# First mixture of experts: experts taken in order of their token counts, four small ones packed into one place

## The chip, the core and the metric

One NeuronCore of a Trainium2 chip runs the whole program. The metric is the device time of one execution in microseconds (us); the median of three runs of the kernel before is 952.01 us (951.53 to 958.26). TensorE is PE in the profile (PEld its weight loads), VectorE is DVE, ScalarE is ACT, GpSimd is POOL, SyncE is SP. SP does no arithmetic here: it issues nearly all weight transfers, in the order of the program.

## What is computed

```python
attn_out = _attn_ref(**attn_kwargs)          # block-causal attention, 4 x 8 heads x 576 x 64
x = attn_out.transpose(0, 2, 1, 3).reshape(2304, 512)
x = _moe_ref(x=x, **moe_kwargs)              # first mixture
return _moe2_ref(x=x, **moe2_kwargs)         # second mixture

def _moe_ref(x, w_skip, w_gate, w1, w2):     # top 1 of 8 experts, some tokens skipped
    do_compute = x @ w_skip > 0
    xc = x[do_compute]
    e_idx = np.argmax(xc @ w_gate, axis=1)
    ...                                      # gate_w: softmax at e_idx
    for e in range(E):
        mask = e_idx == e
        h = np.maximum(xc[mask] @ w1[e], 0.0)          # 512 -> 1024
        y[mask] = gate_w[mask, None] * (h @ w2[e])     # 1024 -> 512
    out[do_compute] = xc + y
```

The second mixture routes every token to two of eight other experts of the same size, with noise added to its router. Everything is float32. Computed from the reference's inputs, 806 tokens enter the first mixture; the experts get 8, 10, 122, 180, 460, 16, 2 and 8 of them.

## The kernel before, in words

The work has three stages on one instruction stream per engine, in an order that the program writes out by hand (`tc.manual_schedule()`): attention; then the first mixture, one *place* of 128 tokens after another; then the second mixture with 592 places per expert. Each row that leaves the first mixture goes through the second router in the place after it.

**Between attention and the first mixture** PE works for the second mixture: `up` and two `down` calls (256 early tokens of expert 0). Woven into them through the `between` arguments are the last steps of the first router (`begin`, `go_on`, `last`), which end with GpSimd scatters of (token, gate) into the list `l1` in DRAM, and `table` and `fullest`, which read the list back, rank the experts (DVE `key`, `keyx`, `keyi`), read two expert numbers into SP registers (`values_load`) and gather more of the list (`ctm`).

**First mixture.** `places` has twelve entries of 128 tokens: one for each expert, three more for the fullest expert and one more for the second fullest (`FULL, NEXT = 3, 1`). An expert's weights are eight transfers of 512 KB: four chunks of the first matrix (to `ring`, three buffers of 2 MB, used as they are) and four of the second (to `ST[4:8]`), which ACT and DVE split into a high and a low part (`W2`, two buffers); the low part of chunk 7 is GpSimd's. Ten expert loads are made (`order`), 40 MB; the first expert's are fixed, so they are issued while attention ends.

One place (`tile1`) on PE is: `cut` (transposes the next place's gathered rows, L161 and ACT L893), `gemm1` half 0 (L1041, f32) with `turn` (L161) and `mm` (L1080) of the second router between, `gemm1` half 1, with the router's `second` steps put in front of the relu (ACT L1045, DVE L1046), and `gemm2` (L1055 to L1057, 24 fp32r products of 512 columns), with the router's `third` after its fifth group. `finish` (DVE L1095 to L1099) writes the rows. On DVE `second` has the line L290 (`atb`); on GpSimd the low part of chunk 7 is L1162; gathers and scatters are L202 and L194.

What exceeds the places is left to a loop behind the second mixture (`one_more`), under a branch that is not taken with these inputs.

Instructions of one engine run in program order, and an engine waits at the first whose operands are not ready. A tile pool opened later on the same memory (`rp`, over `ep`) waits until the old tiles are released: the ring's buffers lie over `x0`, `h0` and `y` of the `up` and `down` calls.

Of the kernel before, what the change touches and what calls it, by code (L numbers as in the profile page):

```python
# [22 lines left out]
E = 8  # L23
# [6 lines left out]
FULL, NEXT = 3, 1  # L30
# [16 lines left out]
def moe_kernel(ctx, tc, q, k, v, w_skip, w_gate, w1, w2, w_gate2, w_noise, noise, w1b, w2b, out):  # L47
# [54 lines left out]
    npad = fiota("npad", [P, 1], [[0, 1]], N, 1)  # L102

# [781 lines left out]
    with ExitStack() as bctx:  # L885
# [11 lines left out]
        with ExitStack() as ectx:  # L897
# [18 lines left out]

            def split0(c):
                raw_split(ST[c], Q0, c, nc.scalar, nc.vector)
                raw_load(ST[c], w1, w2, 1, c)

            Q0 = Obj()
            Q0.w2h, Q0.w2l = Q2
            xg_pool = []
# [9 lines left out]
            def last():  # L933
                counted.extend(counts(C1, "n1"))
                late.L = L[B - 1][:, :, 9:25]
                late.nz = cst.tile([P, 5, E], F32, name="latenz")
                nc.vector.tensor_copy(late.nz, X[B - 1][:, :, D:W])
                late.inv = skip[B - 1]
                late.tok = tok_of(B - 1)
                xctx.close()  # L940
                xg = bctx.enter_context(tc.tile_pool(name="xg", bufs=1, side="right", reuse_waits="tile"))
                x = xg.tile([P, 6, D], F32, name="xg")
                XG.extend(x[:, i, :] for i in range(6))
                x_.append(x)
                nc.gpsimd.memset(x[:, 0:3, :], 0.0)
                lists.append(list_load(l1, 1, x[0:E, 3, :]))

            late, counted, XG, lists, x_ = Obj(), [], [], [], []
            up(WA, x0, h0, ((0, H0),), {1: begin, 2: lambda: go_on(3), 3: last, 4: lambda: split0(KC),
                                        5: lambda: split0(KC + 1), 7: lambda: split0(KC + 2)})  # L950
            tables = []

            def table():
                tok1, idx1, gate1, val1 = token_table(lists[0], 1, "t1", "s")
                nc.gpsimd.memset(x_[0][:, 3:5, :], 0.0)
                for e in range(2):
                    gather(xd, idx1[:, 0, e:e + 1], XG[e], N)
                inv1 = cst.tile([P, 1, E], F32, name="inv1")
                nc.vector.tensor_scalar(inv1, val1, -BIG, BIG, op0=OP.mult, op1=OP.add)
                tables.extend(t[:, 0, :] for t in (tok1, idx1, gate1, inv1))  # L960
                fullest()

            more, fuller = [], []

            def fullest():
# [7 lines left out]
                ni = cst.tile([P, 2], I32, name="fulli")  # L973
                nc.vector.tensor_copy(ni, ki[:, 0:2])
                fuller.extend(nc.values_load(ni[0:1, i:i + 1], engines=(mybir.EngineType.SP,), min_val=0, max_val=E - 1)
                              for i in range(2))
                nf = cst.tile([P, 2], F32, name="fullf")
                nc.vector.tensor_copy(nf, ki[:, 0:2])
                begun = cst.tile([P, E], F32, name="begun")
                own = cst.tile([P, E], F32, name="own")  # L980
                nc.vector.memset(begun, float(P))
                n = FULL + NEXT
                base = cst.tile([P, 2], F32, name="seatb")
                seat = cst.tile([P, n], I32, name="seats")
                for i, tiles_ in enumerate((FULL, NEXT)):
                    nc.vector.tensor_scalar(base[:, i:i + 1], nf[:, i:i + 1], float(R), posc, op0=OP.mult, op1=OP.add)
                    for t in range(tiles_):
                        c = i * FULL + t
                        nc.vector.tensor_scalar(seat[:, c:c + 1], base[:, i:i + 1], float((t + 1) * P), None, op0=OP.add)
                ctm = cst.tile([P, n, 2], F32, name="ctm")  # L990
                for c in range(n):
                    gather(l1, seat[:, c:c + 1], ctm[:, c, :], NROW)
                for i, tiles_ in enumerate((FULL, NEXT)):
                    nc.vector.tensor_scalar(own, e8, nf[:, i:i + 1], float(tiles_ * P), op0=OP.is_equal, op1=OP.mult)
                    nc.vector.tensor_tensor(begun, begun, own, op=OP.add)
                tokm, gatem, invm = (cst.tile([P, n], F32, name=nm + "m") for nm in ("tok", "gate", "inv"))
                idxm = cst.tile([P, n], I32, name="idxm")
                more.extend((begun, ctm, tokm, idxm, gatem, invm))

            def further():  # L1000
# [8 lines left out]
            down(WA, h0, 0, P, known[1][1][:, 0, :], known[1][2][:, 0, :], ep,  # L1009
                 {1: lambda: split0(KC + 3), 3: table})  # L1010
            tok1, idx1, gate1, inv1 = tables
            n1f, n1i = counted
            down(WA, h0, P, P, known[1][1][:, 1, :], known[1][2][:, 1, :], ep, {6: lambda: cut(0, 0, 0)})
        rp = bctx.enter_context(tc.tile_pool(name="rp", bufs=1, reuse_waits="tile"))
        ring = [ST[0:KC]] + [tiles(rp, f"r{i}", KC, F32) for i in range(2)]
        order = [0, 1, 2, fuller[0], 3, 4, 5, fuller[1], 6, 7]
        V = len(order)
        W1 = [ring[i % 3] for i in range(V)]
        places = []
        for j in range(V):  # L1020
            if j in (3, 7):
                for t in range(NEXT if j > 3 else FULL):
                    T = Obj()
                    T.j, T.work = j, t == 0
                    c = t + (FULL if j > 3 else 0)
                    T.gate, T.tok, T.idx, T.inv = (more[i][:, c:c + 1] for i in (4, 2, 3, 5))
                    places.append(T)
            else:
                T = Obj()
                T.j, T.work = j, True  # L1030
                T.gate, T.tok, T.idx, T.inv = (a[:, order[j]:order[j] + 1] for a in (gate1, tok1, idx1, inv1))
                places.append(T)


        def gemm1(j, e, half, between={}):

            s = bank("s", 2 * j + half).rearrange("p (i n) -> p i n", i=4)
# [62 lines left out]

        def tile1(i):

            T = places[i]
            j, k = T.j, i % 2
            work = split_steps(j) if T.work else {}
# [6 lines left out]
            turn, mm, first, second, third = pending(row1, k > 0)  # L1112
# [22 lines left out]
            if j == V - 1:  # L1135
                for c in range(KC):
                    raw_load(ST[c], w1b, w2b, 1, c)
            finish(o, XG[i % 3], T.gate, T.tok, T.idx, T.inv)
# [13 lines left out]
        def split_steps(e):  # L1152

            def step(c):
                src = ST[c].rearrange("p (a d) -> p a d", a=2)
                h, l = (W2[e % 2][i][c - KC] for i in range(2))

                def hi():
                    nc.scalar.activation(h, src, AF.Copy)

                def lo():
                    (nc.gpsimd if c == NCH - 1 else nc.vector).tensor_sub(l, src, h.bitcast(F32))  # L1162

                def load():
                    if e + 2 < V:
                        raw_load(ST[c], w1, w2, order[e + 2], c)
                    else:
                        raw_load(ST[c], w1, w2b, e + 2 - V, c)
                    if 1 <= e < V - 2:
                        raw_load(W1[e + 2][c - KC], w1, w2, order[e + 2], c - KC)  # L1170
                return {"hi": hi, "lo": lo, "load": load}
            return {c: step(c) for c in range(KC, NCH)}

        for c in range(KC):
            raw_load(W1[1][c], w1, w2, 1, c)
        for c in range(KC):
            raw_load(W1[2][c], w1, w2, 2, c)

# [37 lines left out]
        further()  # L1216
        for i in range(len(places)):
            if i == len(places) - 2:
                settled.append(len(put_back))
            if i + 1 < len(places):  # L1220
                cut((i + 1) % 3, (i + 1) % 2, 0)
            if i + 2 < len(places):
                take(places[i + 2].idx, (i + 2) % 3)
            if i == 4:
                over = rest()
            tile1(i)
# [262 lines left out]
```

## Time and profile before

| | |
|---|---|
| median of three runs | 952.01 us |
| profiled execution | 954.42 us, span 952.6 us |
| busy share PE / DVE / ACT / POOL | 93% / 56% / 39% / 45% |
| granted TensorE clock, mean | 0.966 |
| attention and what is woven into it | 0 to 278 us |
| `up`, `down` for the early tokens | 278 to 308.5 us |
| first mixture, twelve places | 308.5 to 510.2 us |
| second mixture | 510 to 952 us |

A granted clock of 1.00 is TensorE's level of 2.4 GHz, 0.50 its level of 1.2 GHz. Times in the rows are counted from the start of the span. Matmul ends are modelled, so the distance from one start to the next tells more than a row's length.

### The profile page before, as it was taken

Reading aid. Unit: us, or ns where it says so; the run is one execution under the profiler, and the core shown is the slowest. Engines: PE = TensorE matmul, PEld = TensorE weight load, DVE = VectorE, ACT = ScalarE, POOL = GpSimd, SP = SyncE. Lnnn points to the kernel's source line nnn. Section 1 sums busy time; section 2 is a strip of 40 time slices with the busy share of each in tenths; the row PEclk is TensorE's granted clock in tenths of the full one; section 3 lists DMA queues with packets and bytes.
Section 4 is the critical chain, followed back from the end, with each engine's and each line's share of the span. In section 5 each row is a group of like instructions: output and inputs, shape, how many; then the busy total and the mean of one; then the engine's idle time right before and its main releaser. Section 6 shows DMA issues by size and latency. Waiting matters only on the chain.

```text
span 952.6 us, 16785 instructions
## 1 busy us (share of the span) xinstructions
PE 887.7 (93%) x6184; PEld 784.5 (82%) x6184; DVE 537.1 (56%) x1464; ACT 370.1 (39%) x664; POOL 433.4 (45%) x326
## 2 busy tenths in 40 slices
PE   6998998898789988899999999999999999999995
PEld 4777776676678877678788899999999999999994
DVE  4666756746355577255766464555546364555631
ACT  4565554544333433133433162242434233343400
POOL 1223254242226546535545341554828465570835
PEclk9999999988799999899997999999999999999998
DMA  6776378351154878338866272564645455560333
GB/s 99 155 148 153 82 153 137 75 119 34 45 207 141 279 277 262 49 112 265 264 199 200 46 226 67 142 123 124 143 104 123 98 141 105 135 144 1 27 34 43
DMA packets 161243, 125.77 MB, mean 132 GB/s; under 512 B 110784, under 2 KB 124864, under 8 KB 161152
## 3 DMA queue, kind: packets, MB, share of 16 engines
q1 hardware_dynamic: 136272, 100.34, 37.6%
q0 software_dynamic: 22448, 23.98, 14.8%
q8 instruction: 50, 0.82, 0.4%
q10 hardware_dynamic: 2432, 0.30, 0.2%
q14 instruction: 41, 0.34, 0.1%
HBM read 104.93 MB, written 23.51 MB: 135 GB/s over the span
## 4 chain that ended last, share of the span: by engine, by line
PE 77%; DVE 11%; issue 3%; ACT 3%; SPq 3%; DMA 2%; another core or an unknown queue 0%; POOLq 0%; DVEq 0%; POOL 0%; ACTq 0%
PE bank L403 22%; PE sums L635 6%; PE bank L1041 5%; PE bank L446 4%; PE bank L447 4%; PE bank L448 4%; PE bank L1285 4%; PE bank L1287 4%; PE bank L1286 4%; PE bank L607 3%; PE seta L556 2%; PE bank L387 2%; DVE atb L290 2%; PE bank L1057 2%; PE bank L701 2%
## 5 line engine op out<-in xcount | busy, mean ns | idle before, releaser
L1295 POOL DMA_INDIRECT out_dram<-y,toq x77 | 150.6, 1956 | 94.3 <-DVE y L1294 75.1
L403 PE MATMUL bank<-xh,w1h 128*128 128x296 f32 (+2 forms) x512 | 123.1, 301 | 0.0
L403 PE MATMUL bank<-xl,w1h 128*128 128x296 f32 (+2 forms) x512 | 122.1, 299 | 0.7 <-DVE xl L391 0.3
L403 PE MATMUL bank<-xh,w1l 128*128 128x296 f32 (+2 forms) x512 | 122.2, 300 | 0.0
L406 ACT ACTIVATE hh<-bank 128x296 fp32r<-128x296 f32 (+2 forms) x128 | 47.8, 413 | 149.2 <-PE bank L403 145.8
L635 PE MATMUL sums<-v,ptS 128*128 128x65 f32 x640 | 94.1, 283 | 9.9 <-remote 5.1
L407 DVE SCALAR_TENSOR_TENSOR hl<-bank,hh 128x296 fp32r<-128x296 f32 (+2 forms) x128 | 54.1, 459 | 77.1 <-ACT hh L406 74.0
L635 PEld LDWEIGHTS sums<-v,ptS 128*128 128x128 f32 x640 | 84.2, 199 | 12.2 <-remote 5.2
L403 PEld LDWEIGHTS bank<-xh,w1h 128*128 128x128 f32 x512 | 88.4, 191 | 0.9 <-ACT xh L390 0.2
L403 PEld LDWEIGHTS bank<-xl,w1h 128*128 128x128 f32 x512 | 87.8, 191 | 1.2 <-DVE xl L391 1.2
L497 ACT ACTIVATE ptS<-bank 128x384 f32<-128x384 f32 (+2 forms) x119 | 56.1, 511 | 82.8 <-PE bank L607 38.9
L403 PEld LDWEIGHTS bank<-xh,w1l 128*128 128x128 f32 x512 | 87.8, 191 | 0.0
L149 ACT ACTIVATE q2h<-st 128x1024 fp32r<-128x1024 f32 x32 | 62.2, 1945 | 61.6 <-PE bank L448 61.6
L202 POOL DMA_INDIRECT rows<-xd,t3x x35 | 35.6, 1018 | 86.0 <-PE bank L387 79.0
L194 POOL DMA_INDIRECT l<-ent,idxb x40 | 42.8, 1070 | 67.3 <-DVE C L185 33.3
L1285 PE MATMUL bank<-hh,q2h 128*128 128x336 f32 x224 | 72.3, 323 | 0.0
L1287 PE MATMUL bank<-hh,q2l 128*128 128x336 f32 x224 | 70.9, 317 | 0.0
L1286 PE MATMUL bank<-hl,q2h 128*128 128x336 f32 x224 | 70.8, 316 | 0.0
L152 DVE TENSOR_TENSOR q2l<-st,q2h 128x1024 fp32r<-128x1024 f32 x32 | 61.2, 1913 | 16.6 <-ACT q2h L149 16.6
L607 PEld LDWEIGHTS bank<-idf,P 128*128 128x128 f32 x320 | 36.4, 147 | 32.2 <-issue 19.1
L446 PE MATMUL bank<-q2h,hh 128*128 128x512 f32 x136 | 54.7, 402 | 0.0
L447 PE MATMUL bank<-q2l,hh 128*128 128x512 f32 x136 | 54.3, 399 | 0.0
(348 smaller groups left out, 1958.2 us busy)
## 6 DMA issues: line engine op xcount, KB each, us to landing
st<-in_moe_w_dram SPq DMA_DIRECT2D x124, 512.0 KB
r<-in_moe_w_dram SPq DMA_DIRECT2D x24, 512.0 KB
out_dram<-zero SPq DMA_DIRECT2D x19, 256.0 KB
kraw<-in_k_dram SPq DMA_DIRECT2D x60, 72.0 KB
qraw<-in_q_dram SPq DMA_DIRECT2D x60, 72.0 KB
v<-in_v_dram SPq DMA_DIRECT2D x64, 64.0 KB
xd<-Xe SPq DMA_DIRECT2D x2, 1024.0 KB
out_dram<-y,toq POOLq DMA_INDIRECT x77
```

What stands on the lines that cost most here:

```text
L149: nc.scalar.activation(h, src, AF.Copy)
L152: on_low.tensor_sub(l, src, h.bitcast(F32))
L403: nc.tensor.matmul(s[i][:, :c1 - c0], a, part[:, c, c0:c1], start=st, stop=sp)
L446: nc.tensor.matmul(o[:n], a, wh, start=f == 0, stop=False)
L447: nc.tensor.matmul(o[:n], a, wl, start=False, stop=False)
L497: nc.scalar.activation(o, i, AF.Copy)
L607: nc.tensor.transpose(pt[:, c:c + P], U.P[:, h, c:c + P], idf)
L635: nc.tensor.matmul(o[:, h, t, :], U.T[h][:, c + j * P:c + (j + 1) * P], vb[:, j, h, :], start=j == 0, stop=j == t)
L1285: nc.tensor.matmul(o[:, :n], wh, a, start=f == 0, stop=False)
L1286: nc.tensor.matmul(o[:, :n], wh, b, start=False, stop=False)
L1287: nc.tensor.matmul(o[:, :n], wl, a, start=False, stop=f == FC - 1)
L1295: st = nc.gpsimd.indirect_dma_start(out=out.rearrange("n (a d) -> (n a) d", d=P), in_=y, in_offset=None, compute_op=OP.add, out_offset=bas ...
```

## The change

The first mixture gets nine places. All eight experts are ranked by count (`ranking`, called in `last`), and the ranks are read into eight SP registers. The four fullest experts get 4, 2, 1 and 1 places (`TILES`); the other four share one place, 32 tokens each (`FEW`), whose products are f32 matmuls of 32 stationary columns, one per expert, written to PSUM partitions 0 to 31, 32 to 63, 64 to 95 and 96 to 127. The shared place's work is eight `few_step` calls, of eight matmuls of 512 columns each: steps 0 to 4 stand between `gemm1` and `gemm2` of places 1 to 4 (`middle`), steps 5 to 7 in `few_place`, which is the seventh of the nine. Their weights (16 MB) come unsplit through `fewb`, `ST[4:8]` and `W1b`. Expert 0's fixed early loads are gone; the first expert's eight loads stand behind the `values_load`s. All nine token lists come by gather (`ctm`), with the three first row gathers in `further`, now inside the first `down`. In `tile1` the relu of half 1 stands in front of `second`, `third` moves one group later, and GpSimd's low part of chunk 7 is made in four pieces.

```diff
-FULL, NEXT = 3, 1
+TILES = (4, 2, 1, 1)
+FEW = 32
...
-            for c in range(T0, NCH):
-                raw_load(ST[c], w1, w2, 0, c)
             for t in range(T0):
                 turn2(x0, ST[t], t * P, P, "s")
-            for c in range(T0):
-                raw_load(ST[c], w1, w2, 0, c)
...
-                nc.gpsimd.memset(x[:, 0:3, :], 0.0)
-                lists.append(list_load(l1, 1, x[0:E, 3, :]))
+                ranking()
+                nc.gpsimd.memset(x[:, 0:4, :], 0.0)
...
+                rank.extend(nc.values_load(ni[0:1, i:i + 1], engines=(mybir.EngineType.SP,), min_val=0, max_val=E - 1)
+                            for i in range(E))
+                for c in range(NCH):
+                    raw_load(ST[c], w1, w2, rank[0], c)
...
+                for c in [0, 1, n - 1] + list(range(2, n - 1)):
+                    gather(l1, seat[:, c:c + 1], ctm[:, c, :], NROW)
...
+                for c, g in ((0, 0), (1, 1), (sum(TILES), 3)):
+                    gather(xd, idxm[:, c:c + 1], XG[g], N)
+
+            up(WA, x0, h0, ((0, H0),), {1: begin, 2: lambda: go_on(3), 3: last})
...
+            down(WA, h0, 0, P, known[1][1][:, 0, :], known[1][2][:, 0, :], ep, {4: further})
+            down(WA, h0, P, P, known[1][1][:, 1, :], known[1][2][:, 1, :], ep, {3: reached, 7: lambda: cut(0, 0, 0)})
...
+        W1b, fewb = (tiles(rp, f"r{i}", KC, F32) for i in range(2))
+        few = rp.tile([P, FC, P], F32, name="few")
+        W1 = [ST[0:KC], W1b, ST[0:KC], W1b]
+        fewbuf = [fewb, ST[KC:], ST[KC:], fewb, ST[KC:], ST[KC:], fewb, W1b]
...
+        def few_step(i):
+            if i in (0, KC):
+                sums[:] = [bank("s", 2 + half) for half in range(2 if i == 0 else 1)]
+            for half in range(2):
+                for g in range(P // FEW):
+                    cols = slice(g * FEW, (g + 1) * FEW)
+                    f = i if i < KC else 2 * (i - KC) + half
+                    nc.tensor.matmul(sums[half if i < KC else 0][cols], few[:, f, cols],
+                                     fewbuf[i][g][:, half * 512:half * 512 + 512], start=f == 0,
+                                     stop=f == (KC if i < KC else FC) - 1, skip_group_check=True)
...
+                    for a in range(2):
+                        for d in (slice(0, D // 2), slice(D // 2, D)):
+                            nc.gpsimd.tensor_sub(l[:, a, d], src[:, a, d], h[:, a, d].bitcast(F32))
...
+        splits = {0: lambda: split_steps(ST[KC:], 1, lambda c: few_chunk(1, c)),
+                  2: lambda: split_steps(fewb, 0, lambda c: few_chunk(3, c)),
+                  4: lambda: split_steps(fewb, 1, lambda c: few_chunk(6, c)),
+                  7: lambda: split_steps(fewb, 0, lambda c: None),
+                  8: lambda: split_steps(ST[KC:], 1, lambda c: raw_load(ST[c], w1, w2b, 1, c))}
...
+        def middle(i):
+            if i == 0:
+                few_rows()
+            if i == 1:
+                few_step(0)
+                seconds(1, fewb)
+                few_step(1)
+                load_few(2)
+            if i == 2:
+                few_step(2)
+                load_few(4)
+            if i == 3:
+                few_step(3)
+                few_relu()
+                seconds(2, fewb)
+                load_first(2, ST[0:KC])
+            if i == 4:
+                few_step(4)
+                load_few(5)
+            if i == 5:
+                load_few(7)
...
-            gemm1(k, j, 1, {3: second})
+            gemm1(k, j, 1)
+            second()
             extra(i)
-            o = gemm2(j, {4: third})
-            pick("lo", 6)
+            if i == 0:
+                pick("lo", 6)
+            middle(i)
+            o = gemm2(j, {5: third})
+            if i > 0:
+                pick("lo", 6)
...
+        def few_place(i):
...
+            turn()
+            few_step(5)
+            for c in range(KC, NCH):
+                raw_load(ST[c], w1, w2b, 0, c)
+            mm()
+            first()
+            few_step(6)
+            seconds(3, fewb)
+            second()
+            few_step(7)
+            load_first(3, W1b)
...
-        for c in range(KC):
-            raw_load(W1[1][c], w1, w2, 1, c)
-        for c in range(KC):
-            raw_load(W1[2][c], w1, w2, 2, c)
+        load_few(0)
+        load_first(1, W1b)
```

`seconds(j, buf)` and `load_first(j, buf)` load the second and first matrix of the expert of rank j (four chunks each), `load_few(i)` one 512 KB chunk of each of the four small experts. `few_rows` and `few_turn` transpose the shared place's rows and its hidden layer, `few_relu` is its relu.

## Rows read from the trace of the kernel before

**Rows 1.** The page, shares of the span and the chain that ended last.
```profile
PE 887.7 (93%) x6184; PEld 784.5 (82%) x6184; DVE 537.1 (56%) x1464; ACT 370.1 (39%) x664; POOL 433.4 (45%) x326
PE 77%; DVE 11%; issue 3%; ACT 3%; SPq 3%; DMA 2%; another core or an unknown queue 0%; POOLq 0%; DVEq 0%; POOL 0%; ACTq 0%
```
**Rows 2.** Windows, one per place: stretch, length, busy per engine (instructions), clock, DMA share, GB/s.
```profile
308.51:324.88 16.37, 15.18 (x107) 13.26 (x106) 11.25 (x35) 6.62 (x11) 9.73 (x7) 1.00 0.86 267
...
357.71:376.00 18.29, 15.81 (x114) 13.61 (x113) 14.94 (x62) 6.67 (x12) 10.66 (x8) 1.00 0.80 280
376.00:398.05 22.05, 18.47 (x108) 14.61 (x107) 6.05 (x35) 3.01 (x7) 13.04 (x14) 0.85 0.35 75
398.05:412.73 14.68, 14.68 (x108) 13.35 (x106) 5.60 (x31) 2.90 (x7) 6.63 (x7) 1.00 0.25 38
412.73:431.28 18.55, 16.72 (x107) 14.37 (x106) 10.94 (x34) 6.58 (x11) 8.58 (x8) 0.91 0.56 183
...
sum 201.72, PE 186.49 PEld 161.73 DVE 123.66 ACT 71.76 POOL 107.27; mean PE 15.54 PEld 13.48 DVE 10.30 ACT 5.98 POOL 8.94
```
**Rows 3.** Timeline of the first place: start, length, engine, line, tiles, shapes, count, [idle before].
```profile
312.95 0.96 PE L1080 MATMUL bank<-wcat,xt 128*128 128x16 f32 x8
313.77 3.82 PE L1041 MATMUL bank<-xt,st 128*128 128x128 f32 x32
317.34 0.48 PE L1055 MATMUL bank<-q2h,ht 128*128 128x512 f32 x1
321.57 0.50 PE L1055 MATMUL bank<-q2h,ht 128*128 128x512 f32 x1 [1.19 <-ACT ht L1045]
318.17 2.54 POOL L1162 TENSOR_TENSOR w2l<-st,w2h 128x1024 fp32r<-128x1024 f32 x1 [2.19 <-ACT w2h L1159]
318.91 1.81 DVE L290 TENSOR_TENSOR atb<-mib,pinv 128x2 f32<-128x2 uint32 x1
320.83 0.20 ACT L295 ACTIVATE e<-d 128x1 f32<-128x1 f32 x1 [2.75 <-DVE d L291]
```
**Rows 4.** PE's waits, 295 to 520 us: who waited for whom, total, times, longest.
```profile
PE bank L1055 <- ACT ht L1045: 8.8, 8, 1.8
```
**Rows 5.** Timeline in attention: products that fill only part of TensorE's columns.
```profile
69.52 0.89 PE L652 MATMUL sums<-v,ptS 128*64 128x65 f32 x18
70.16 0.45 PE L562 MATMUL setb<-kt,qt 64*64 64x288 f32 x1
71.37 0.87 PE L607 MATMUL bank<-idf,P 128*128 128x128 f32 x6
```
**Rows 6.** Timeline ahead of the first mixture: router list, ranking, gathers.
```profile
288.34 0.17 PE L338 MATMUL bank<-C,onesb 128*128 128x8 bf16 x1
293.82 1.16 POOL L194 DMA_INDIRECT l<-ent,idxa  x1 [0.30 <-issue]
296.24 0.34 SPq L362 DMA_DIRECT2D xg<-l  x1
300.72 0.17 DVE L974 CAST fulli<-keyi 128x2 int32<-128x2 uint32 x1
302.36 0.82 SPq L131 DMA_DIRECT2D r<-in_moe_w_dram  x2
307.02 1.01 POOL L202 DMA_INDIRECT ctm<-l,seats  x1 [0.30 <-issue]
309.60 0.17 DVE L1003 COPY tokm<-ctm 128x4 f32<-128x4 f32 x1
```
**Rows 7.** POOL's waits, 295 to 520 us.
```profile
POOL l L194 <- DMA next<-l,seat: 3.8, 1, 3.8
```
**Rows 8.** Windows of 16 to 18 us and of 4 us, columns as in the second group.
```profile
310.00:328.00 18.00, 16.81 (x124) 14.89 (x123) 11.13 (x36) 6.82 (x12) 10.77 (x8) 1.00 0.93 307
497.00:514.00 17.00, 15.04 (x103) 13.16 (x101) 12.30 (x42) 7.17 (x12) 11.00 (x9) 0.96 0.53 155
392.00:396.00 4.00, 4.00 (x11) 2.14 (x10) 1.50 (x8) 0.60 (x1) 0.00 (x0) 0.50 0.00 0
```

More of the change, by code (lines that the diff above doesn't have):

```diff
@@ L944, in last, with ranking @@
                 x_.append(x)
-                nc.gpsimd.memset(x[:, 0:3, :], 0.0)
-                lists.append(list_load(l1, 1, x[0:E, 3, :]))
[L948 to L965, printed above, removed]
+                ranking()
+                nc.gpsimd.memset(x[:, 0:4, :], 0.0)
+            late, counted, XG, x_ = Obj(), [], [], []
+            more, rank = [], []
+            def ranking():
                 key = cst.tile([P, E], F32, name="key")
@@ L972, in fullest @@
                 nc.vector.max_index(ki, kx, key)
[L973 to L978, printed above, removed]
+                ni = cst.tile([P, E], I32, name="ranki")
@@ L980, in fullest @@
                 own = cst.tile([P, E], F32, name="own")
[L981 to L994, printed above, removed]
+                nc.vector.memset(begun, 0.0)
+                for i in range(E):
+                    nc.vector.tensor_scalar(own, e8, nf[:, i:i + 1], float(TILES[i] * P if i < len(TILES) else FEW),
+                                            op0=OP.is_equal, op1=OP.mult)
@@ L995, in fullest @@
                     nc.vector.tensor_tensor(begun, begun, own, op=OP.add)
[L996 to L998 removed]
+                more[0] = begun
             def further():
@@ L1029, in moe_kernel @@
+        few = rp.tile([P, FC, P], F32, name="few")
+        W1 = [ST[0:KC], W1b, ST[0:KC], W1b]
+        fewbuf = [fewb, ST[KC:], ST[KC:], fewb, ST[KC:], ST[KC:], fewb, W1b]
+        V = len(TILES)
+        places = []
+        for j, tiles_ in enumerate(TILES):
+            for t in range(tiles_):
                 T = Obj()
-                T.j, T.work = j, True
-                T.gate, T.tok, T.idx, T.inv = (a[:, order[j]:order[j] + 1] for a in (gate1, tok1, idx1, inv1))
+                T.j, T.d, c = j, len(places), len(places)
+                T.x, T.xT = XG[c % 3], c % 2
+                T.gate, T.tok, T.idx, T.inv = (more[i][:, c:c + 1] for i in (4, 2, 3, 5))
@@ L1032, in moe_kernel, with load_first, load_second, load_few @@
                 places.append(T)
+        T = Obj()
+        T.j, T.x, c = None, XG[3], len(places)
+        T.gate, T.tok, T.idx, T.inv = (more[i][:, c:c + 1] for i in (4, 2, 3, 5))
+        dense = list(places)
+        places.insert(sum(TILES[:2]), T)
+        def load_first(j, buf):
+            for c in range(KC):
+                raw_load(buf[c], w1, w2, rank[j], c)
+        def load_second(j, buf, c):
+            raw_load(buf[c - KC], w1, w2, rank[j], c)
+        def load_few(i):
+            for g in range(P // FEW):
+                raw_load(fewbuf[i][g], w1, w2, rank[V + g], i)
@@ L1101, in tile1, with after @@
+        def after(i):
+            if i == 3:
+                few_turn()
+            if i == 7:
+                for c in range(KC):
+                    raw_load(ST[c], w1b, w2b, 1, c)
         def tile1(i):
             T = places[i]
-            j, k = T.j, i % 2
-            work = split_steps(j) if T.work else {}
+            j, k = T.j, T.xT
+            work = splits[i]() if i in splits else {}
             def pick(kind, *cs):
@@ L1110, in pick @@
                         work[c][kind]()
-            turn, mm, first, second, third = pending(row1, k > 0)
+            turn, mm, first, second, third = pending(row1, i % 2 > 0)
             gather(noise, T.idx, nz, N)
@@ L1129, in tile1 @@
             pick("lo", 7)
-            gemm1(k, j, 1, {3: second})
+            gemm1(k, j, 1)
+            second()
             extra(i)
-            o = gemm2(j, {4: third})
-            pick("lo", 6)
-            pick("load", 7, 6)
-            if j == V - 1:
-                for c in range(KC):
-                    raw_load(ST[c], w1b, w2b, 1, c)
-            finish(o, XG[i % 3], T.gate, T.tok, T.idx, T.inv)
+            if i == 0:
[4 more added lines that the diff above has]
+                pick("lo", 6)
+            pick("load", 7, 6)
+            after(i)
+            finish(o, T.x, T.gate, T.tok, T.idx, T.inv)
+        def few_place(i):
+            T = places[i]
+            turn, mm, first, second, third = pending(row1, i % 2 > 0)
+            gather(noise, T.idx, nz, N)
+            turn()
+            few_step(5)
+            for c in range(KC, NCH):
+                raw_load(ST[c], w1, w2b, 0, c)
[6 more added lines that the diff above has]
+            load_first(3, W1b)
+            extra(i)
+            third()
+            finish(sums[0], T.x, T.gate, T.tok, T.idx, T.inv)
         def rest():
```

108 lines of the change are left out of this document (61 added, 47 removed).

## The prediction

> **What bounds the kernel now.** I read the page first: PE is busy 93% of the span and carries 77% of the chain that ended last [rows 1]. So time is gained where PE does less, or where it stands. Then the windows of the twelve places: they take 201.7 us, 186.5 of them busy on PE [rows 2]. A place without splitting takes 14.68 us with PE never idle; one with splitting 16.37, of which 1.19 is PE waiting in `gemm2` [rows 2, 3]. That wait occurs eight times, 8.8 us in all, always for the relu of half 1 [rows 4]. Its cause is order: ACT's little exponential of the router (L295) stands in front of the relu, waits for DVE's `atb`, and that takes 1.81 us beside GpSimd's 2.54 us subtraction [rows 3]. Three places are out of the pattern: 18.29 us where the router of the last 640 tokens burdens DVE (14.94 us busy), 22.05 and 18.55 us where PE stood or ran slowly [rows 2]. Transfers reach 307 GB/s at a 0.93 share and are asked for at 155 GB/s near the end [rows 8], so they don't bound the stage now.
>
> **Dense places.** Eight instead of twelve. Places 1, 3 and 5 split nothing: 3 x 14.7. Places 0, 2, 4, 7 and 8 split: 16.37 less the 1.19 wait, 15.2, five times. With the relu in front, ACT no longer waits for `atb`; what is late next is `ohb` for `third`, which has one more group of `gemm2` before it and, with four GpSimd pieces, a shorter block on `atb`. I take no wait. The late router stays where it was, with an excess of 18.29 - 16.4 = 1.9. Sum 44.1 + 76.0 + 1.9 = 122.0 us. The cutting in pieces adds a few starts on GpSimd, which is busy 8.9 of 16.8 us per place [rows 2]; they lie beside PE's work.
>
> **The shared place.** An f32 matmul is two instructions; 32 of 128 columns take 317.34 - 313.77 = 3.57 us, 0.112 each [rows 3], so one of 512 columns takes 0.447. A `few_step` is eight matmuls, 16 instructions. No row shows parts of 32 columns. The nearest are parts of 64 columns: 18 instructions of 65 columns start within 0.64 us, where one after another would take 18 x 0.057 = 1.03; eight of 288 columns take 1.21 us to the next product, instead of 8 x 0.252 = 2.0 [rows 5]. Both are about two at a time, which fills the array. Bounds for a step: four at a time 4 x 0.447 = 1.8 us, two 3.6, one 7.15. I take four, because two parts of 64 columns fill the same 128 columns as four of 32, and 0.2 for going in and out of the narrow form: 2.0 us, eight steps 16 us. The Trainium skill ("TensorE: Matmul & The Clock Gate", Part 3) gives three such column parts at 2.38 times one; by it I estimate a step at 1.8 x 3 / 2.38 + 0.2 = 2.5 us, 4 us more in the whole; no row here shows three parts. The rest of the shared place: twelve transposes at 0.112 (the rows once, the hidden layer twice), 1.3 us; `turn` and `mm`, 0.45 and 0.82 (312.95 to 313.77 [rows 3]); about 0.9 of waiting for its router chain, which has only two steps beside it instead of `gemm1` and `gemm2`. Sum 16 + 1.3 + 1.3 + 0.9 = 19.5 us.
>
> So the stage is 122.0 + 19.5 = 141.5 us instead of 201.7: 60.2 us less, PE's work of about three places (45 us) and most of the 15 us in which PE stood.
>
> **What the new start costs.** The list's last scatter is issued at 293.82 to 294.98, and the list can be read from 296.24 [rows 6]. Nine gathers now follow, each 1.01 + 0.30: to 308.0. Landing takes 1.6 us (308.03 to DVE's first use, 309.60 [rows 6]) up to 3.8 [rows 7]; I take 1.6, then 0.7 for DVE's five small steps: 310.3. The memset of the row tiles, behind the gathers on POOL, is done by then. Row gather 0 is issued to 311.4, gather 1 to 312.7; landing 2.7, the middle of the two ends: 315.4. `cut` of place 1, which PE meets ahead of place 0, so starts at 315.4 instead of 308.51: 6.9 us later, with ends at 5 (both landings 1.6) and 10. In those 7 us PE stands for lack of rows, with f = 7 of `down` and all behind it queued. After PE had been standing near 390 us, the granted clock was 0.50 from 392 to 396 [rows 8], PE busy throughout; 3.4 us at half speed give back 1.7 us of work, which I add (ends 0 and 3.5). DVE's `further` waits for the gathers too; behind it stand `y`, seventeen small steps of `reached` and the second `y`. These matter to SP alone: `fewb` cannot be loaded until the second `y` has been scattered. On SP, two register reads take 302.36 - 300.89 = 1.5 us [rows 6], eight about 5.5; the count's product is done at 288.5, ranking follows in some 2 us, so the first expert's loads start near 296 and, 4 MB at 307 GB/s, are there by 312, hidden by the gathers. Dropping the early fixed loads frees transfers at 266 to 281 us, where I cost and credit nothing.
>
> **Transfers.** Fourteen groups of 2 MB follow, each 6.8 us at 307 GB/s plus some 2 us of issue, through `fewb`, `ST[4:8]`, `ST[0:4]` and `W1b`; a group may start when the step that read its buffer is done, and SP stops at the first that may not. I followed each. Tightest are step 1 (ready about 341, wanted 343), step 3 (372 against 375) and the last expert's: its second matrix at 434 and its first at 441, both within 1 us of what wants them. I cost this at nothing, and put 5 us into the range; if cover fails at one place, it is `few_step` or ACT's split that waits, with `gemm2` behind it.
>
> **The sum.** -60.2 + 6.9 + 1.7 = -51.6 us on the profiled execution's 954.4: 902.8. That execution stands 2.4 us over the median, so 900.4 against 952.0, say 901 (5.4% less). What follows is the same work as before.
>
> **Rivals.**
> - *Parts run two at a time*, because their moving columns share a supply: steps of 3.8 us, 14 us more, 915. For it: the rows never show more than two. Against: those two already fill all columns. Chance 0.16.
> - *One at a time*: steps of 7.35, 43 us more, 944, hardly a gain. Rows 5 speak against. 0.05.
> - *The unexplained slowing stays.* The 22.05 us place held 7.4 us beyond 14.68 with ACT and DVE idle too [rows 2], and the 18.55 us place 2.2. If it belongs to the late router's scatters, it returns at the same place; with a wait or two for weights of the tight list above, 8 to 15 us more, 910 to 917. 0.14.
> - *Slower than before: reloading becomes the bound.* With two or three buffers reused in turn, every step waits for its 2 MB and SP's order keeps later loads back. It decides where the fourteen groups and `w2b`, 31.5 MB, take longer than 315 to 520 less some start: under about 160 GB/s. Then the stage ends after 520 us, at 965 or more. For it: the 155 GB/s near the end [rows 8]. Against: there little was asked for, and 307 was reached under load. 0.03.
> - *The capacities don't hold*, and the loop behind the second mixture runs with eight loads and a place for each expert over: at least 4 MB at 307 GB/s and 15 us of PE, some 30 us each, to 930, and beyond 952 with two experts over. The counts 460, 180, 122, 16, 10, 8, 8, 2 fit 512, 256, 128, 128 and four times 32. 0.02.
>
> **How the numbers follow.** The forecast has 0.60, its own range 891 (start at its low end, the relu's order giving the splitting places 14.7 too, steps hidden in waits) to 910 (start and clock at their upper ends, the skill's price of a step). The range of 891 to 926 takes in the two-at-a-time case and the slowing with its waits: 0.54 + 0.14 + 0.12 = 0.80. A measurement of this kernel can tell about 1% (9.5 us) from no change: faster 0.60 + 0.16 + 0.14, same 0.05 (one at a time), slower 0.05.
>
> **What would show it.** Right: nine stretches of PE, 14.7 to 15.2 us plus 2 us where a step stands in them; the idle time in front of L1055's successor gone; `cut` for place 1 near 315; 16 step instructions within 2 us, starting in fours. Wrong: a step of 3.6 or 7 us; PE idle behind weight transfers in front of a step or of `gemm1`; a first place that starts after 320 us.

## The result and the profile after

The changed kernel takes 915.93 us (median; 913.77 to 921.39), the kernel before 954.03 (951.53 to 958.26) in the same series: a ratio of 0.9605, interval 0.9546 to 0.9664, 38.1 us less. The forecast was 901, the range 891 to 926. The profiled execution is the longest of the four (921.39 us, span 919.6); 6.7 us of it lie in attention, ahead of all that was changed: `up` starts at 287.79 instead of 281.07. In another profiled execution of the changed kernel it starts at 264.9, where the kernel before with its router steps exchanged, on the same chip, has 271.3; so I don't put the 6.7 us down to the change.

The page, to be held against [rows 1]: PE has 37 us less to do and the same share.

```profile
PE 851.0 (93%) x5912; PEld 745.2 (81%) x5912; DVE 485.7 (53%) x1360; ACT 340.8 (37%) x621; POOL 405.7 (44%) x329
```

Windows of the places, columns as in [rows 2]; the stretch from 434.90 is the shared place. As in [rows 2], place 0 begins with the `cut` in front of it; the last window ends behind the last product.

```profile
325.44:343.18 17.74, 16.94 (x112) 15.26 (x111) 9.52 (x30) 7.17 (x12) 8.00 (x9) 0.91 0.91 288
...
361.59:378.30 16.71, 16.71 (x124) 13.83 (x122) 10.99 (x50) 6.93 (x13) 8.75 (x9) 1.00 0.89 301
...
397.20:419.78 22.58, 19.28 (x123) 15.85 (x123) 8.08 (x37) 7.56 (x13) 12.05 (x14) 0.92 0.75 231
...
434.90:444.52 9.62, 8.11 (x62) 2.91 (x63) 3.36 (x23) 1.22 (x4) 3.19 (x4) 1.00 0.93 219
444.52:462.09 17.57, 15.65 (x110) 13.36 (x110) 10.21 (x47) 6.91 (x11) 7.76 (x9) 1.00 1.04 391
...
sum 151.06, PE 142.21 PEld 116.33 DVE 73.12 ACT 46.38 POOL 70.17; mean PE 15.80 PEld 12.93 DVE 8.12 ACT 5.15 POOL 7.80
```

By these windows the stage takes 151.1 us. Up to the second mixture's first transposes (478.12), where the 201.7 us of [rows 2] end, it takes 152.7; 141.5 and 1.7 for the clock were forecast. The splitting place with one step (361.59) takes 16.71, forecast 17.2. Two are well over the forecast: 22.58 us from 397.20, with PE idle for 3.3 and the clock at 0.92, and 17.57 from 444.52, with transfers at their full share.

The start, from a timeline (columns as in [rows 3]):

```profile
303.12 1.07 POOL L207 DMA_INDIRECT ctm<-l,seats  x1 [1.89 <-DVE hl L412]
313.71 1.01 POOL L207 DMA_INDIRECT ctm<-l,seats  x1 [0.30 <-issue]
318.80 0.17 DVE L996 COPY tokm<-ctm 128x9 f32<-128x9 f32 x1 [15.08 <-DMA ctm<-l,seats]
319.79 1.02 POOL L207 DMA_INDIRECT xg<-xd,idxm  x1 [3.25 <-issue]
323.28 1.09 PE L166 MATMUL bank<-idf,xg 128*128 128x128 f32 x4 [10.36 <-DMA xg<-xd,idxm]
324.02 0.78 PE L451 MATMUL bank<-w2h,hh 128*128 128x512 f32 x1
325.44 1.05 PE L166 MATMUL bank<-idf,xg 128*128 128x128 f32 x4
326.29 3.10 PE L1076 MATMUL bank<-xt,st 128*128 128x128 f32 x16
```

Nine gathers stand between the list and its first use, as forecast; PE stands 10.36 us for the rows. From the start of `up` to the first product of `gemm1` (L1076) it takes 38.51 us, before 27.88: 10.6 more. From that product to the second mixture's first transposes it takes 151.83 us, before 201.28: 49.4 less. Behind the first mixture the two executions are alike: 441.5 us from there to the end, before 442.4. So the profiled difference is +6.7 + 10.6 - 49.4 - 0.9 = -33.0 us.

The steps (L1051) in the same view, and what follows them:

```profile
352.19 1.92 PE L1051 MATMUL bank<-r,few 128*32 128x512 f32 x16
353.93 1.90 PE L1051 MATMUL bank<-st,few 128*32 128x512 f32 x16
355.76 0.50 PE L1090 MATMUL bank<-q2h,ht 128*128 128x512 f32 x1
```

From start to start a step takes 1.74 and 1.83 us. Last, PE's waits in the stage, where [rows 4] had 8.8 us for the relu:

```profile
PE bank L1115 <- ACT xt L1110: 1.9, 1, 1.9
...
PE bank L1051 <- DMA r<-in_moe_w_dram: 1.0, 1, 1.0
PE bank L1090 <- ACT ht L1080: 0.9, 1, 0.9
```

The relu's wait is down to 0.9 us, once.

### The profile page after: what moved, and what is told of

It reads as the page before. It is cut to its first block, busy times and chain, and to the rows that moved or that the text cites. A ratio compares the mean times of both kernels' runs of the same rounds, so it can differ in the third digit from the quotient of the medians.

```text
span 919.6 us, 16133 instructions
## 1 busy us (share of the span) xinstructions
PE 851.0 (93%) x5912; PEld 745.2 (81%) x5912; DVE 485.7 (53%) x1360; ACT 340.8 (37%) x621; POOL 405.7 (44%) x329
## 4 chain that ended last, share of the span: by engine, by line
PE 58%; DMA 3%; DVE 2%; issue 1%; ACT 1%; POOL 1%; SPq 0%; POOLq 0%; ACTq 0%; DVEq 0%
PE bank L408 22%; PE bank L1076 6%; PE bank L1387 4%; PE bank L1389 4%; PE bank L1388 4%; PE bank L451 4%; PE bank L452 3%; PE bank L453 3%; DMA r<-in_moe_w_dram 2%; PE bank L392 2%; PE bank L1090 1%; PE bank L1092 1%; PE bank L1091 1%; PE bank L166 1%; PE bank L1115 1%
## 5 line engine op out<-in xcount | busy, mean ns | idle before, releaser
L640 PE MATMUL sums<-v,ptS 128*128 128x65 f32 x640 | 97.7, 290 | 10.9 <-remote 5.4
L640 PEld LDWEIGHTS sums<-v,ptS 128*128 128x128 f32 x640 | 88.0, 207 | 13.1 <-issue 6.1
L154 ACT ACTIVATE q2h<-st 128x1024 fp32r<-128x1024 f32 x28 | 58.0, 2072 | 61.6 <-PE bank L453 61.6
L199 POOL DMA_INDIRECT l<-ent,idxb x38 | 39.9, 1050 | 61.2 <-DVE C L190 28.3
L157 DVE TENSOR_TENSOR q2l<-st,q2h 128x1024 fp32r<-128x1024 f32 x28 | 56.4, 2014 | 15.6 <-ACT q2h L154 15.6
L612 PE MATMUL bank<-idf,P 128*128 128x128 f32 x320 | 50.5, 298 | 4.4 <-issue 1.6
```

Source lines behind the costliest of these rows:

```text
L157: on_low.tensor_sub(l, src, h.bitcast(F32))
L612: nc.tensor.transpose(pt[:, c:c + P], U.P[:, h, c:c + P], idf)
L640: nc.tensor.matmul(o[:, h, t, :], U.T[h][:, c + j * P:c + (j + 1) * P], vb[:, j, h, :], start=j == 0, stop=j == t)
```

## The experiments

Twelve kernels ran in three groups of four, each beside the kernel before, which took 921.1, 925.9 and 964.9 us there; times are compared within a group. The groups ran on the chips numbered 8, 3 and 15; for the first series no number is on record. Places are counted from 0 and, from here on, measured from the first product of `gemm1` to the next place's.

**First group: is the time where the forecast puts it?**

*few_wide*: all 128 stationary columns in a step.

```diff
-nc.tensor.matmul(sums[half if i < KC else 0][cols], few[:, f, cols],
+nc.tensor.matmul(sums[half if i < KC else 0], few[:, f, :],
```

> The changed kernel with one edit: each of the four products of a few_step uses all 128 rows of the shared place as stationary columns and writes all 128 PSUM partitions, so the shared place's rows come out as a mixture of four experts (that part is wrong); instructions and loads stay the same in number. Theory (four narrow products run at the same time): a step grows from 1.8 us to 16 x 0.447 = 7.15 us, eight steps +43 us, of which a few us may hide waits: 950 to 960 us. Rival (the steps are paced by their weight loads, and the narrow form gives nothing): under +15 us, below 930.

925.25 us, 1.0027 (0.9986 to 1.0068) of before, some 37 us over its three neighbours. Its timeline:

```profile
331.06 7.03 PE L1051 MATMUL bank<-r,few 128*128 128x512 f32 x16
337.94 7.03 PE L1051 MATMUL bank<-st,few 128*128 128x512 f32 x16
```

6.88 us a step against 1.74 to 1.83: the parts of 32 columns run four at a time, and without that the whole gain is gone.

*relu_back*: the old order of relu and router.

```diff
-gemm1(k, j, 1)
-second()
+gemm1(k, j, 1, {3: second})
 extra(i)
...
-o = gemm2(j, {5: third})
+o = gemm2(j, {4: third})
```

> The changed kernel with the old order of relu and router steps: second in front of the relu of half 1, third after the fifth group. Theory (the exchange takes away ACT's wait for DVE in places that have no few_step behind gemm1): about 1 us in places 0, 7 and 8 each, nothing where a few_step covers it, together +2 to +4 us (918 to 920). Rival (the pieces on GpSimd alone removed the wait): no difference, within 1 us.

887.24 us, 0.9647 (0.9608 to 0.9685). The theory's 2 to 4 us don't show: the ratio is level with the unchanged 0.963 of the next group, and the stage takes 143.3 us against 142.9 there. PE waits for the relu once, 1.9 us. With steps between `gemm1` and `gemm2` and pieces on GpSimd, the old order costs little; which of the two covers it, this run doesn't tell.

*early_three*: three list columns are gathered first, then their rows, then the other six columns.

```diff
+seek1(0, range(3))
+seek1(1, range(2))
...
-for c, g in ((0, 0), (1, 1), (sum(TILES), 3)):
+for c, g in ((0, 0), (1, 1), (2, 3)):
     gather(xd, idxm[:, c:c + 1], XG[g], N)
+seek1(1, range(2, len(sets[1])))
...
+if i == 0:
+    further(1)
+    take(dense[2].idx, 2)
...
```

> The changed kernel with a split of the list gathers: the memset of the row tiles goes in front, the gathers for places 0, 1 and the shared one come first and have their own tiles, so that the first row gathers wait for three list gathers instead of nine; the other six follow, two of them ahead of the row gathers. Theory (the start is held by the chain of nine gathers, their landing and the memset): the first rows land 7 to 9 us earlier, and with PE's stop shorter the half clock goes too: -7 to -10 us. Rival (the first expert's weights, issued behind eight register reads, are what the first place waits for next): -0 to -3 us, with PE waiting for a weight transfer ahead of the first gemm1.

888.94 us, 0.966 (0.9614 to 0.9705): no gain, where the theory expected 7 to 10 us; the wait for weights that the rival named isn't there either. The start is 34.15 us, 4.4 less than in relu_back, but place 0 takes 21.06 us (17.07 in w2b_last), for PE waits in it:

```profile
318.41 0.50 PE L1110 MATMUL bank<-q2l,ht 128*128 128x512 f32 x1 [1.61 <-DVE den L306]
323.43 1.11 PE L166 MATMUL bank<-idf,xg 128*128 128x128 f32 x4 [2.04 <-DMA xg<-xd,idxm]
```

The rows of the next place, asked for behind the second set of lists, are late in their turn.

*w2b_last*: the second mixture's four early loads behind the last expert's first matrix instead of ahead of it.

```diff
-for c in range(KC, NCH):
-    raw_load(ST[c], w1, w2b, 0, c)
 mm()
...
 load_first(3, W1b)
+for c in range(KC, NCH):
+    raw_load(ST[c], w1, w2b, 0, c)
```

> The changed kernel with the four loads of the second mixture's second matrix, in the shared place, moved behind the loads of the last expert. Theory (place 7's relu waits on ACT behind the splits of the last expert's second matrix, which land late because 2 MB of the second mixture go first): about 2 us less in place 7, -1.5 to -3 us. Rival (place 7 is long for the router steps and places of the next mixture): no difference, within 1 us.

888.26 us, 0.9659 (0.9617 to 0.9701). The windows of places 7 and 8:

```profile
414.73:429.06 14.33, 14.33 (x105) 13.06 (x104) 9.98 (x45) 6.68 (x11) 8.48 (x10) 1.00 1.02 381
429.06:445.74 16.68, 14.33 (x104) 12.78 (x102) 11.65 (x47) 6.08 (x10) 8.72 (x9) 1.00 0.79 270
```

Place 7 has PE never idle, 2.9 us less than the 17.26 that the next group's unchanged kernel shows; place 8 gives 0.9 back (there 15.82), and the time doesn't show the rest. So the late weights were four loads that nobody needed yet, ahead in SP's order.

**Second group: the change once more, and its parts.**

*after_again*: the changed kernel as it is.

> The changed kernel itself, once more, as the measure for the others of this call, since chips differ in their times. Theory: the same ratio to the kernel before as at first, 0.955 to 0.967; and if the slow stretch in place 4 (22 us) belongs to that chip's execution and not to the late router, place 4 takes 16 to 17 us here, otherwise 22 again.

887.23 us, 0.963 (0.9587 to 0.9673). Windows of places 0, 4 and 5 with the shared one, of 7, and the sum:

```profile
302.42:319.53 17.11, 16.48 (x112) 14.82 (x111) 8.72 (x31) 7.17 (x12) 8.41 (x9) 0.93 0.87 276
...
372.84:389.49 16.65, 16.65 (x124) 13.84 (x123) 8.24 (x29) 6.69 (x11) 11.84 (x14) 1.00 1.03 293
389.49:412.21 22.72, 21.88 (x171) 16.05 (x170) 9.68 (x58) 4.23 (x11) 11.08 (x11) 1.00 0.92 230
412.21:429.47 17.26, 14.99 (x106) 12.96 (x105) 9.91 (x45) 6.92 (x11) 7.75 (x9) 1.00 1.05 396
...
sum 142.87, PE 137.38 PEld 113.51 DVE 74.51 ACT 46.51 POOL 71.24; mean PE 17.17 PEld 14.19 DVE 9.31 ACT 5.81 POOL 8.90
```

142.9 us, where 143.2 were forecast with the clock. The near match is in part luck: places 7 and 8 take 2.7 us more than forecast, places 1 to 6 take 3.2 less. Place 4 takes 16.65, not 22.2: the same program has the slow stretch in one series and not in another.

*before_exchange*: the kernel before, with the new order of relu and router and GpSimd's four pieces.

```diff
-gemm1(k, j, 1, {3: second})
+gemm1(k, j, 1)
+second()
...
-o = gemm2(j, {4: third})
+o = gemm2(j, {5: third})
...
-(nc.gpsimd if c == NCH - 1 else nc.vector).tensor_sub(l, src, h.bitcast(F32))
+if c < NCH - 1:
+    nc.vector.tensor_sub(l, src, h.bitcast(F32))
+    return
+for a in range(2):
+    for d in (slice(0, D // 2), slice(D // 2, D)):
+        nc.gpsimd.tensor_sub(l[:, a, d], src[:, a, d], h[:, a, d].bitcast(F32))
```

> The kernel before with only two parts of the change: relu of half 1 in front of second (third one group later), and GpSimd's low part in four pieces. Theory (ACT's wait for atb stands on the path in eight places, 8.8 us): -6 to -9 us of the time before, a ratio of 0.990 to 0.994. Rival (the wait turns into one for ohb ahead of third): within 3 us of the kernel before.

913.22 us, 0.9879 (0.9837 to 0.9922): 11 us less than before by the ratio, a little more than the 6 to 9 expected. Its first places and the sum:

```profile
298.86:313.51 14.65, 14.65 (x108) 13.34 (x107) 9.62 (x35) 6.68 (x11) 10.00 (x10) 1.00 0.90 268
313.51:328.19 14.68, 14.68 (x108) 13.36 (x107) 9.89 (x35) 6.79 (x11) 8.84 (x10) 1.00 0.90 319
...
sum 178.28, PE 175.88 PEld 159.62 DVE 114.08 ACT 72.83 POOL 110.44; mean PE 14.66 PEld 13.30 DVE 9.51 ACT 6.07 POOL 9.20
```

A splitting place takes what one without splitting takes. From 178.3 to the 142.9 of after_again are 35.4 us: that is what the rest of the change, the shared place above all, brings to the stage, and 10.0 of it go to the start (27.5 to 37.5).

*few_unloaded*: the small experts' loads only for step 0 (14 MB fewer; the later steps use what lies in the buffers).

```diff
 for g in range(P // FEW):
-    raw_load(fewbuf[i][g], w1, w2, rank[V + g], i)
+    if i == 0:
+        raw_load(fewbuf[i][g], w1, w2, rank[V + g], i)
...
-raw_load(fewbuf[i][c - KC], w1, w2, rank[V + c - KC], i)
+return
```

> The changed kernel without seven of the eight groups of loads for the shared place (14 MB); its steps multiply by what lies in the buffers, so the shared place's rows are wrong. Theory (transfers lie beside PE's work; only the shared place's last step and place 7's split see them): -1 to -4 us against the changed kernel. Rival (reloading paces the stage): -10 us or more.

892.13 us, 0.9648 (0.9594 to 0.9702), not below after_again, and the 1 to 4 us of the theory don't show: the stage takes 142.3 us against 142.9, and place 7 stays at 17.26. The 14 MB are hidden.

*early_four_w2b*: as early_three with four columns first, the other five asked for right behind the first rows and used at the end of place 0; and w2b_last.

```diff
-seek1(0, range(3))
-seek1(1, range(2))
+seek1(0, range(4))
...
-for c, g in ((0, 0), (1, 1), (2, 3)):
+for c, g in ((0, 0), (1, 1), (2, 3), (3, 2)):
     gather(xd, idxm[:, c:c + 1], XG[g], N)
-seek1(1, range(2, len(sets[1])))
+seek1(1, range(len(sets[1])))
...
 finish(o, T.x, T.gate, T.tok, T.idx, T.inv)
+if i == 0:
+    further(1)
...
```

> The changed kernel with two edits: the list gathers for places 0, 1, 2 and the shared one come first, behind the memset, in tiles of their own, and the row gathers for all four follow at once, while the other five list entries are read at the end of place 0; and the second mixture's loads in the shared place go behind the last expert's. Theory (the start costs 10 us and place 7 some 2 to 3 because of this order): -5 to -9 us against the changed kernel. Rival (what comes earlier at the start is lost again in place 0, which waits for rows or runs at the lower clock): -3 us or less, all of it in place 7.

885.71 us, 0.9585 (0.9546 to 0.9623): 1.5 us under after_again, within the intervals. Place 7 takes 14.33, the start 33.62 (3.9 less), place 0 21.32 (4.2 more). The timeline shows why:

```profile
306.59 1.01 POOL L207 DMA_INDIRECT ctm<-l,seats  x1 [0.30 <-issue]
307.91 1.64 POOL L457 DMA_INDIRECT out_dram<-y,t0o  x1 [0.30 <-issue]
...
313.84 1.07 POOL L207 DMA_INDIRECT nz<-in_moe_noise_dram,idxm  x1 [0.30 <-issue]
314.93 2.81 POOL L1170 TENSOR_TENSOR q2l<-st,q2h 128x256 fp32r<-128x256 f32 x4
319.01 0.79 PE L1109 MATMUL bank<-q2l,ht 128*128 128x512 f32 x1 [2.85 <-DVE q2l L1166]
```

POOL issues without a gap; its pieces come last, DVE's part of the split behind them, and PE waits 2.85 us for that. Behind the wait PE works at a granted clock of 0.50 from 319 to 325 us: its busy time in place 0 is 18.47 us, in after_again's 16.48. So both halves of the rival hold, the wait and the lower clock.

**Third group: which half of the exchange, and is the slow place the chip's?**

*before_again* (the kernel before), *before_relu* (of before_exchange's edit only the order) and *before_pieces* (only the pieces).

> The kernel before itself, profiled again. Theory (the two slow places of its first profile, 22.05 and 18.56 us, belong to that execution): places of 14.7 and 15.6 to 16.6 us only, 18.3 where the late router is, the stage about 190 us instead of 201.3. Rival (they belong to the kernel): 22 and 18.5 us again, stage 199 to 203. Time against itself: ratio 1.

> The kernel before with the exchange alone: relu of half 1 in front of second, third one group later; GpSimd's low part in one piece. Theory (order alone caused the wait for the relu): most of the gain of both edits together, -7 to -11 us, splitting places 14.7 us. Rival (atb, still held by GpSimd's 2.5 us piece, now delays ohb and with it third): places of 15 to 16 us, -2 to -5 us.

> The kernel before with the pieces alone: GpSimd's low part of chunk 7 in four, old order of relu and second. Theory (order alone caused the wait): relu waits as before for atb, which is shorter by about 1 us, -2 to -6 us. Rival (the block by GpSimd is the cause): as much as both edits together, -9 to -13 us.

966.67 us, 0.9991 (0.9945 to 1.0038); 946.17, 0.9848 (0.9776 to 0.992); 951.3, 0.9863 (0.982 to 0.9906). Either half alone gives about what both gave: by the ratio 14.7 us for the order and 13.2 for the pieces, where the theory of before_pieces had 2 to 6. So neither the order nor the long subtraction alone makes the wait; it needs both. In before_pieces DVE's `atb`, 1.81 us in [rows 3], stands beside GpSimd's pieces so:

```profile
321.02 3.00 POOL L1167 TENSOR_TENSOR w2l<-st,w2h 128x256 fp32r<-128x256 f32 x4 [0.87 <-ACT w2h L1159]
321.77 0.16 DVE L290 TENSOR_TENSOR atb<-mib,pinv 128x2 f32<-128x2 uint32 x1
```

The Trainium skill ("SBUF — State Buffer", "SBUF: two separate sides") has DVE and GpSimd share a pair of ports that one instruction locks for its whole length; among its cases is a DVE instruction with two inputs in SBUF beside a GpSimd one that reads SBUF. The trace agrees: in [rows 3] `atb`, with two such inputs, ends at 320.72, GpSimd's subtraction at 318.17 + 2.54 = 320.71; with pieces `atb` runs 0.16 us, at the end of the first quarter (321.02 + 3.00 / 4 = 321.77).

Place 4 of these three, one window each, in their order:

```profile
381.80:403.66 21.86, 18.86 (x109) 14.15 (x108) 6.07 (x36) 3.01 (x7) 12.68 (x14) 0.84 0.36 74
```

```profile
377.39:400.96 23.57, 17.77 (x108) 14.62 (x107) 6.46 (x37) 3.01 (x7) 13.20 (x14) 0.86 0.39 88
```

```profile
375.04:397.09 22.05, 17.98 (x108) 14.40 (x107) 6.04 (x36) 3.01 (x7) 12.37 (x14) 0.85 0.46 91
```

I had held the 22.05 us of [rows 2] for a matter of that one execution; here it stands in all three, and before_again's stage takes 204.9 us, not 190. It is in none of the seven profiles of the first two groups that have places without wide steps (14.67 in before_exchange, 16.64 to 16.65 in the changed kernel's variants). That theory fell: the stretch goes with the series, so with the chip or with something else that set the series apart. The 18.55 us place did not return (17.05 in before_again).

*four_then_five*: as early_four_w2b, but the five lists are asked for in place 0, behind the pieces, and used in place 1.

```diff
-seek1(1, range(len(sets[1])))
...
 extra(i)
+if i == 0:
+    seek1(1, range(len(sets[1])))
+if i == 1:
+    further(1)
+    take(dense[3].idx, 0)
```

> As early_four_w2b, but the other five list gathers are issued in place 0 behind GpSimd's low part, and read in place 1, so that they no longer stand in front of GpSimd's work for place 0. Theory (in early_four_w2b place 0 lost 4 us because GpSimd's low part came late, behind five list gathers): place 0 takes 17 us, -6 to -9 us against the changed kernel, a ratio of 0.952 to 0.957. Rival (place 0 is held by the weights and its lower clock): place 0 again 20 us or more, a ratio like 0.9585.

928.61 us, 0.9616 (0.9559 to 0.9673): no better than the change itself (0.9605, 0.963). Its profile, of its longest execution (933.47 us), shows where the gain went in that one. Places 0 and 1, a part of place 1, and PE's wait in it:

```profile
329.13:346.16 17.03, 16.35 (x111) 14.68 (x111) 8.78 (x31) 7.17 (x12) 10.38 (x11) 0.94 0.80 234
346.16:373.54 27.38, 22.07 (x140) 17.53 (x139) 6.89 (x41) 2.90 (x7) 7.39 (x8) 0.88 0.56 195
356.00:363.00 7.00, 7.00 (x38) 6.92 (x37) 1.89 (x9) 0.42 (x2) 0.00 (x0) 0.58 0.00 0
355.20 1.89 PE L1132 MATMUL bank<-wcat,xt 128*128 128x16 f32 x8 [4.87 <-ACT xt L1127]
```

The start takes 35.0 us and place 0 17.03, as the theory said, which speaks for POOL's backlog as what held it. But place 1 takes 27.38, where after_again has 18.42: PE and ACT stand in it, and PE then works at the lower clock. Place 4 takes 19.65, where after_again has 16.65. Both look like the slow stretch of this series, now in place 1 too, right behind the five gathers that were moved.

## Why the prediction was right, and which terms were off

The direction and the mechanism held: three places fewer, the shared place's products four at a time, the relu's wait nearly gone, the sum of the weights hidden. 915.9 is 14.9 us over the forecast and where the rivals "two at a time" (915) and "the slowing stays" (910 to 917) stood. The time alone couldn't tell them apart; the steps do: 1.8 us, not 3.8. That the number fell into the range is in part luck. The forecast's own range, 891 to 910, was missed; the range reaches to 926 for the rivals' sake. One of these, "the unexplained slowing stays", given 0.14, is what this execution shows beside the forecast mechanism: the slowing at the same place and two waits for weights. Term by term, on the profiled execution:

- **Step of the shared place**, 2.0 taken, 1.74 to 1.83 measured. The nearest rows, read as two parts at a time though they give 1.6 and 1.7 (1.03 / 0.64 and 2.0 / 1.21), had been extended to four, and few_wide confirms it: 6.88 / 1.8 is 3.8. The Trainium skill's 2.38 for three parts ("TensorE: Matmul & The Clock Gate", Part 3) would have given 2.5; here the measurement decides.
- **Dense places and the slowing**, the step that failed most: "60.2 us less, PE's work of about three places (45 us) and most of the 15 us in which PE stood". The 22.05 us place was entered as 14.7 or 15.2 like the others, and returned as 22.2, where 16.65 stand without it: 5.5 us. Its timeline after the change:

```profile
402.20 0.57 PE L1076 MATMUL bank<-xt,r 128*128 128x128 f32 x3 [0.34 <-issue]
403.60 0.39 PE L1076 MATMUL bank<-xt,r 128*128 128x128 f32 x2 [0.83 <-issue]
405.87 1.06 PE L1115 MATMUL bank<-wcat,xt 128*128 128x16 f32 x8 [1.88 <-ACT xt L1110]
406.78 5.45 PE L1076 MATMUL bank<-xt,r 128*128 128x128 f32 x32
```

  PE stands with nothing to wait for that the profile shows, ACT is late as well, and 32 products then take 5.45 us instead of 3.82 [rows 3], at a granted clock of 0.80, 0.50 and 0.85 in the windows of 2 us from 406. Why, stays open; that it isn't the change's, before_again shows.
- **Relu's wait**, 8.8 us credited; before_exchange measures 11 for removing it. I kept splitting places at 15.2, they take 14.65.
- **The start**, +6.9 taken, +10.6 measured (10.0 in the second group). The step "Landing takes 1.6 us ...; I take 1.6" failed: from the last gather's end (314.72) to `tokm` it is 4.1 us, over the upper bound of 3.8 [rows 7]. It had company, as a window of the profile after shows; before, transfers moved 52 GB/s at 308 to 310 us, where the 1.6 us of [rows 6] were read. In after_again it took 3.0, with transfers at 321 to 369 GB/s; load and the count of gathers, nine instead of four, were not told apart.

```profile
315.00:317.00 2.00, 0.00 (x0) 0.00 (x0) 0.00 (x0) 0.00 (x0) 1.54 (x1) 0.51 0.98 338
```

  And "`cut` of place 1, which PE meets ahead of place 0" left out what PE meets ahead of that: `cut` of place 0 and f = 7 of `down`, 2.2 us at half clock (323.28 to 325.44). The 1.7 us for the clock covered `gemm1` alone; it came from 3.4 us at half speed, a length that no row shows ([rows 8] has 4 us). Measured, the half clock costs 1.1 us of those 2.2, and about 1.5 in the window of place 0 (0.91 over its 16.94 busy us).
- **Transfers**, "I cost this at nothing". Two were late: a step of the shared place waited 1.0 us for its chunk, and at one of the points named as tightest, the last expert's second matrix, ACT waited in place 7:

```profile
451.09 1.06 ACT L1144 ACTIVATE w2h<-r 128x1024 fp32r<-128x1024 f32 x1 [2.61 <-DMA r<-in_moe_w_dram]
```

  The late split cost place 7 2.9 us, which w2b_last takes away, with 0.9 of it back in place 8. few_unloaded shows that it is the order of the loads, not their sum.

So: attention +6.7, start +3.7, slowing +5.5, late weights about +3 make 18.9 us, against 18.6 between the profiled 921.4 and the 902.8 forecast. What else differs, the shorter steps and the 0.9 us less behind the stage above all, nearly cancels.

Open: what the slow stretch is; and whether a shorter start can be kept. early_three and early_four_w2b start 4 us sooner and lose as much in place 0; for the latter POOL's backlog is shown; in four_then_five's profile it is gone, but the time is lost there to what looks like the slow stretch of its series. It was not run in a series without that stretch.

## What to carry to other kernels

Small groups of rows can share TensorE if each gets its own 32 stationary columns: four products of 128 x 32 x 512, here in f32, then cost about as much as one, provided their weights stream in behind other work. Price a gather on a busy machine by a landing seen on a busy one (here 3.0 to 4.1 us, where 1.6 had been read), and follow the order of the waiting engine up to the very instruction that waits. A stretch that the profile doesn't explain is not a gain to be booked: keep it in the sum, or ask first whether it returns.

## What the runs showed of the hardware

- The same kernel took 921, 926, 954 and 965 us in four series, on three chips at least. The slow stretch in place 4 (3 to 9 us) is in all six profiles of the first and the last series and in none of the seven named above. Ratios (0.9605 and 0.963) travel, times don't.
- In all six, the stretch begins 5 to 13 us into a run of nine or more GpSimd indirect transfers issued 0.30 us apart (373.69 to 391.06 in the profile before, with PE's first pauses behind 385; 341.53 to 353.05 in four_then_five, PE standing from 350). Not every such run has one, and in the two other series none has: before_exchange has twenty in a row, from 357.62 to 384.09, and no pause of PE. So the run of transfers goes with the stretch, but doesn't make it alone; no experiment took it away.
- At the border to the second mixture PE runs at half clock in some executions though it is fully busy, here of the changed kernel in its first series and of after_again:

```profile
484.00:488.00 4.00, 4.00 (x20) 4.00 (x20) 1.01 (x5) 0.80 (x3) 0.00 (x0) 0.50 0.04 12
```

```profile
452.00:458.00 6.00, 6.00 (x54) 5.95 (x53) 4.33 (x27) 1.84 (x6) 0.09 (x1) 1.00 0.01 3
```

  PE was busy for 4.9 us of the 8 before the first stretch, for 4.6 of the 6 before the second. The part behind the stage takes 441.5 us in the one and 436.1 in the other. All fourteen profiles divide so: in four the granted clock stays at 1.00 through the border, and 435.5 to 437.1 us follow; in ten it falls to 0.50, and 440.0 to 442.5 follow. So 5 us hang on it, as much as the edits above were meant to move.
